# Sparse attention with a mixture of experts: product 1 in seven sub-products, output sums in three halves, sub-products spread over a step

## The chip, the cores and the metric

The kernel runs on one core of a Trainium2 chip. The metric is the time of one execution on the device in microseconds (us): the median of three runs of the kernel before is 2161.44 us, the lowest 2160.73, the highest 2161.88. The core's engines are TensorE (PE in the profile, its weight loads are PEld), VectorE (DVE), ScalarE (ACT), GpSimd (POOL) and SyncE (SP), which here issues nearly all DMAs. PE writes its results into PSUM banks; DVE and ACT read them from there.

## The reference

Block-sparse attention, whose output feeds a mixture of eight experts. The change lies in the second part.

```python
def _moe_ref(x, w_gate, w1, w2):          # x: 3072 x 512, w1: 8 x 512 x 1024, w2: 8 x 1024 x 512
    logits = x @ w_gate
    ...
    out = np.zeros((N, D), dtype=np.float32)
    for e in range(E):
        h = np.maximum(x @ w1[e], 0.0)
        ye = h @ w2[e]
        out += P[:, e:e + 1] * ye
    return out
```

All arrays are float32, and float32 accuracy is kept: each operand is held as a high and a low float16 part, and each product is three matmuls (high by high, high by low, low by high).

## The kernel before

**Items.** The second part runs over 32 items: eight experts times four batches of 768 rows (`NI = NE * B`), item `i` being expert `i // 4`, batch `i % 4`. Stage 1 of an item is `relu(x @ w1)`, stage 2 multiplies by `w2` and adds to the batch's sum. Stage 2 of item i is interleaved with stage 1 of item i+1; the main loop at the end calls that a step, and below it is "a step" too.

**Seven products.** Both stages split their matrices in 2 x 2 blocks and use the seven products of Strassen's method (in Winograd's form) in place of eight. In stage 1 a product, numbered 0 to 6, is made for one quarter `qi` of its output rows at a time: two chunks of the inner dimension times three matmuls, each 128x384. In stage 2 a product is three steps (`ci`) of 4 x 3 matmuls of 128x256.

**Sub-products.** From item 8 on (`FIRST_FINE = 2 * B`) product 0 of stage 1 is itself split by the same method into seven sub-products (`fine`, L1491). A sub-product is six matmuls of 128x192, so product 0 costs 7 x 6 = 42 of these, where in the plain form it takes 4 x 6 = 24 of 128x384. They need sums of blocks of w1 (`w1f_sum`, split into `w1f`, once per expert) and of x (`xpf`, made once per batch by `queue_fine_x` and kept in DRAM as `xfd`). They run one item ahead: those of item i+1 stand between the products of item i, in its last two quarters (`QFINE = 2`), those of item 8 alone at the head of its own stage 1. Their results, the pair `a1` of four blocks, are what the other products are added to.

**The other engines in stage 1.** DVE adds each product's PSUM bank to the running sums (`comb`, L1485). ACT writes the float16 high part of each hidden block `h` (L1596) and the relus; the low part is made by DVE from PSUM (L1601), by DVE for product 4 (L1607), or by POOL for products 2, 5 and 6 (L1607, `LOPE`). POOL also makes four sums per quarter (L1661 and L1298). ACT takes the high parts of those sums from POOL, in program order.

**Order.** A class `Slots` holds work that is waiting and, at every `tick`, releases what its count of costs lets through: urgent work (parts of h, the POOL sums), and lazy work (the weights of the next expert: scaling on ACT, sums on POOL at L1291 and L1316, splits on ACT and DVE at L1276 and L1280). `need` forces work out before its first use. The framework's scheduler then settles the order on each engine; engines run their queue in order.

**DMA.** SP's queue carries, per item, the loads of x blocks (L263, `xp`), of `xpf` (L1425), the store and load of the batch's sum (`keep_acc`, L1169, and `fetch_acc`, L1172; 1536 KB each way) and, per expert, the raw w1 and w2 (L202, 2048 KB each, one buffer for both).

**Buffers.** Eight `upool` tiles for temporaries, three `apool` tiles for the pairs, four PSUM banks for stage 1 (`ps_h`) and four for stage 2 (`ps_y`), two whole sums in SBUF (`accs`).

## Time and profile before

| | |
|---|---|
| median of three runs | 2161.44 us |
| the profiled execution | 2162.28 us, of which its span is 2160.5 us |
| DVE, ACT, POOL busy over the span | 1680.3, 1223.6, 1401.6 us |
| matmuls over the span | 19228 |
| first and last matmul of the sub-products (L1513) | start at 827.5 and 2069.3 us |

The attention part fills roughly the first 470 us; the items follow. The page of the profile gives busy times and shares of the span, then 40 slices of 54 us each, the chain of work that ended last, and the costliest groups; the other views used below are groups by line and shape, waits, windows (busy time of each engine in a stretch) and timelines. A matmul's row in a timeline has its start and a duration that includes its way through the array, so the pace is read from one start to the next.

### The profile page before, as it was taken

To read this page: it belongs to the slowest core of one execution; us is meant where nothing else is said; L and a number is where in the kernel's file an instruction comes from. 1 tells how busy PE (TensorE), PEld (TensorE's weight loads), DVE (VectorE), ACT (ScalarE), POOL (GpSimd) and SP (SyncE) were. 2 spreads that over 40 slices of the span, in tenths; PEclk is the share of its full clock that TensorE was granted. 3 is DMA by queue.
4 is the path that set the end of the run, shared out by engine and by line. 5 is a ranking of instruction groups with operands and counts; after the bars stand their busy time and mean duration, and the time that the engine had idled before them with its cause. 6 is when DMAs were issued, how large, how long until landed. Compare 5 with 4: busy or idle time off the path is not lost.

```text
span 2160.5 us, 48393 instructions
## 1 busy us (share of the span) xinstructions
PE 2126.5 (98%) x19228; PEld 1617.8 (75%) x19228; DVE 1680.3 (78%) x3116; ACT 1223.6 (57%) x2352; POOL 1401.6 (65%) x1550
## 2 busy tenths in 40 slices
PE   6999999999999999999999999999999999999999
PEld 4777776677777777777777777777777777777777
DVE  8889998777867677877787778777877787778765
ACT  5888888666465556554554455445544454455332
POOL 5667778567458675867575747575757575757443
PEclk9999999999999999999999999999999999999999
DMA  6757796143144334343434343434343434343331
GB/s 173 188 128 176 170 209 146 39 138 112 63 154 157 132 125 164 125 156 118 157 118 157 118 157 118 157 118 157 118 157 118 157 118 157 118 157 125 118 104 52
DMA packets 208312, 293.10 MB, mean 136 GB/s; under 512 B 133820, under 2 KB 152276, under 8 KB 200916
## 3 DMA queue, kind: packets, MB, share of 16 engines
q1 hardware_dynamic: 207520, 289.97, 43.0%
q8 instruction: 150, 2.46, 0.5%
q14 instruction: 78, 0.64, 0.1%
q10 hardware_dynamic: 564, 0.03, 0.0%
HBM read 195.59 MB, written 62.91 MB: 120 GB/s over the span
## 4 chain that ended last, share of the span: by engine, by line
PE 88%; DVE 5%; POOL 3%; ACT 2%; issue 1%; DMA 0%; POOLq 0%; ACTq 0%; DVEq 0%
PE py L1712 39%; PE p L1580 34%; PE u L834 3%; PE t L769 2%; PE t L772 2%; PE m L736 2%; PE m L739 2%; DVE top L745 2%; PE fy L1513 2%; PE fz L1513 1%; PE fx L1513 1%; ACT pe L777 1%; DVE vl L645 1%; POOL s L1661 0%; DVE pl L787 0%
## 5 line engine op out<-in xcount | busy, mean ns | idle before, releaser
L1712 PEld LDWEIGHTS <-h 128*128 128x128 f16 x8064 | 787.8, 98 | 144.6 <-issue 0.5
L1712 PE MATMUL py<-w2p,h 128*128 128x256 f16 x4608 | 571.1, 273 | 0.0
L1661 POOL TENSOR_TENSOR s<-a,u 128x384 f32<-128x384 f32 x128 | 146.8, 1147 | 578.1 <-ACT a L1658 578.0
L1736 DVE SCALAR_TENSOR_TENSOR acc<-py,spare,acc 128x256 f32<-128x256 f32 (+1 forms) x588 | 300.4, 515 | 145.5 <-PE py L1712 134.3
L1712 PE MATMUL py<-vault,h 128*128 128x256 f16 x3456 | 410.6, 273 | 0.4 <-DVE vault L1280 0.4
L1596 ACT ACTIVATE h<-p 128x384 f16<-128x384 f32 x384 | 186.4, 485 | 249.6 <-DVE p L1485 249.1
L1580 PEld LDWEIGHTS <-attic 128*128 128x128 f16 x2016 | 196.5, 98 | 105.0 <-issue 0.4
L1601 DVE SCALAR_TENSOR_TENSOR h<-p,h 128x384 f16<-128x384 f32 x384 | 211.2, 550 | 51.0 <-ACT h L1596 20.0
L1485 DVE SCALAR_TENSOR_TENSOR a<-p,a 128x384 f32<-128x384 f32 x384 | 211.1, 550 | 37.9 <-PE p L1580 33.9
L1580 PE MATMUL p<-attic 128*128 128x384 f16 x1152 | 214.9, 326 | 0.2 <-DVE a L1485 0.2
L745 DVE TENSOR_REDUCE top<-m 128x1 f32<-128x768 f32 x192 | 181.9, 950 | 31.1 <-PE m L739 29.9
L777 ACT ACTIVATE pe<-t,qk 128x768 int32<-128x768 f32 x192 | 172.6, 901 | 58.9 <-PE t L772 46.2
L1580 PEld LDWEIGHTS <-arena 128*128 128x128 f16 x1440 | 140.2, 98 | 75.4 <-issue 1.7
L1580 PEld LDWEIGHTS <-w1p 128*128 128x128 f16 x1344 | 131.1, 98 | 69.6
L1485 DVE SCALAR_TENSOR_TENSOR p<-p,u 128x384 f32<-128x384 f32 x256 | 143.0, 559 | 44.6 <-PE p L1580 44.0
L1298 POOL TENSOR_TENSOR r<-s,r 128x384 f32<-128x384 f32 x128 | 155.8, 1217 | 10.0
L1580 PE MATMUL p<-arena,attic 128*128 128x384 f16 x864 | 162.1, 326 | 0.0
L1580 PE MATMUL p<-arena 128*128 128x384 f16 x864 | 158.9, 326 | 1.2 <-DVE a L1485 0.8
L791 POOL TENSOR_SCALAR pl<-pe 128x768 f16<-128x768 uint16 x126 | 109.2, 869 | 67.5 <-ACT pe L777 58.8
L1607 DVE TENSOR_TENSOR h<-s,h 128x384 f16<-128x384 f32 x128 | 112.8, 881 | 40.0 <-ACT h L1596 38.4
L834 PE MATMUL u<-vq,pl 128*128 128x65 f16 x1152 | 142.5, 193 | 1.3 <-POOL pl L791 0.9
L1580 PE MATMUL p<-arena,w1p 128*128 128x384 f16 x768 | 143.7, 326 | 0.0
(236 smaller groups left out, 4312.1 us busy)
## 6 DMA issues: line engine op xcount, KB each, us to landing
arena<-xd SPq DMA_DIRECT2D x128, 384.0 KB, 3.9
accd<-acc SPq DMA_DIRECT2D x28, 1536.0 KB, 5.8
acc<-accd SPq DMA_DIRECT2D x28, 1536.0 KB, 6.4
attic<-xd SPq DMA_DIRECT2D x96, 384.0 KB, 3.7
r<-in_moe_w_dram SPq DMA_DIRECT2D x14, 2048.0 KB, 9.0
xpf<-xfd SPq DMA_DIRECT2D x24, 384.0 KB, 3.1
arena<-in_q_dram SPq DMA_DIRECT2D x16, 384.0 KB, 4.2
arena<-in_k_dram SPq DMA_DIRECT2D x16, 384.0 KB, 4.7
```

The lines of the kernel that those rows point to most:

```text
L745: nc.vector.tensor_reduce(out=tops[n][:, c : c + 1], in_=sc[:, :S], axis=AX.X, op=ALU.max)
L777: nc.scalar.activation(pe, sc[:, :S], AF.Exp, bias=EXP_SHIFT, scale=qk[n // 2][3])
L834: nc.tensor.matmul(uv[:, c, :n], lhsT=l[:, c * P : (c + 1) * P], rhs=w[:, h, kc, :n], start=(kc == 0 and c == 0 and m == 0), stop=(kc == N ...
L1298: nc.gpsimd.tensor_tensor(out=out, in0=x, in1=y, op=ALU.subtract)
L1485: nc.vector.scalar_tensor_tensor(out=t, in0=ps, scalar=HDOWN, in1=other, op0=ALU.mult, op1=ALU.add)
L1580: nc.tensor.matmul(ps, lhsT=w1ps[i // B][p][:, l, kc, fs], rhs=xp[p][:, r, kc], start=(kc == 0 and m == 0), stop=(kc == KH - 1 and m == 2),)
L1596: nc.scalar.activation(h[:, 0], src, AF.Relu if relu else AF.Copy)
L1601: nc.vector.scalar_tensor_tensor(out=h[:, 1], in0=src, scalar=0.0, in1=h[:, 0], op0=ALU.max, op1=ALU.subtract,)
L1607: eng.tensor_tensor(out=h[:, 1], in0=src, in1=h[:, 0], op=ALU.subtract)
L1661: nc.gpsimd.tensor_tensor(out=s1, in0=a1, in1=u3, op=ALU.add)
L1712: nc.tensor.matmul(py, lhsT=hs[i, p, kc][:, l, tsl], rhs=w2p[p][:, r, kc], start=(old is None and kc == 0 and m == 0), stop=(kc == KF // 2 ...
L1736: nc.vector.scalar_tensor_tensor(out=dst, in0=src, scalar=c, in1=dst, op0=ALU.mult, op1=ALU.add)
```

## The change

Four things are done.

**Product 1 too is made of seven sub-products** from item 8 on, also one item ahead. `fine` now has 14 steps: seven for product 0 (PSUM banks `fx`, `fy`, `fz`) and seven for product 1 (`gx`, `gy`, `gz`). The result of product 1 lies in a new pool `rpool` (three tiles), started by three additions on POOL (`base`: the first sub-product plus product 0's blocks) and finished by six `comb`s on DVE. Stage 1 of an item then begins with the relu of that result and the high part of h for product 0, both on ACT, and has five products per quarter in place of six; the low part for product 0 goes from DVE to POOL (`lop`). Four more sums of w1 per expert on POOL (into the tile `s3` that is free by then), one more split into `w1f_1`, twice as many block sums of x (made in items 2 to 5 in place of 4 to 7). The two products' inputs `xpf` share one tile: `load_pieces(i, 1)` is issued after step 5 (sub-product 4 of product 0), and step 9 (sub-product 5 of product 1) is its first reader.

**The sub-products are spread** over a step by the table `BETWEEN`: one or two after a named product of quarters 1 to 3. Item 8's own run in the step before, from blocks that `load_first` brings into two tiles that are free then.

**The sums lie in three halves**: `accs` has three tiles of half a sum, two for the lower halves and one for all upper halves. The upper half is stored after product 4 of stage 2, its last writer, and the next batch's upper half is fetched right behind; 768 KB each.

**Room**: `upool` has six tiles, since the temporaries for product 1 are gone.

```diff
-NU = 8
+NU = 6
...
-    FINE_P = NP
+    FINE_P = (NP, NP + 1)
...
-    xfd = [dram.tile([P, 2, 4, TQ], F16, name=f"xfd_{b}") for b in range(B)]
+    xfd = [
+        [dram.tile([P, 2, 4, TQ], F16, name=f"xfd_{b}_{p}") for p in range(2)]
+        for b in range(B)
+    ]
...
+    rpool = mpool("rpool", 3)
...
-    accs = [big.tile([P, NC, DM], F32, name=f"acc_{b}") for b in range(2)]
+    accs = [big.tile([P, CH, DM], F32, name=f"acc_{n}") for n in range(3)]
...
     def acc(t):
-        return accs[t // NC % 2][:, t % NC]
+        b, c = divmod(t, NC)
+        return accs[2 if c >= CH else b % 2][:, c % CH]
+
+    def move_acc(b, j, keep):
+        out_, in_ = accd[b][:, j * CH : (j + 1) * CH], accs[2 if j else b % 2]
+        if not keep:
+            out_, in_ = in_, out_
+        nc.sync.dma_start(out=out_, in_=in_)
...
-        finer["w"] = right.tile([P, 2, 4, FQ], F16, name="w1f")
+        finer["w"] = [right.tile([P, 2, 4, FQ], F16, name=f"w1f_{p}") for p in range(2)]
...
         one(0, a[0, 0])
+        fine_sums(0, tmps[0], a[0, 0])
         if e == 2:
-            split_finer()
+            split_finer(0)
         queue_sum(a[0, 0], a[1, 0], a[0, 0], ("w1", e, 5))
         one(1, a[0, 1])
+        one(6, s3)
+        fine_sums(1, tmps[1], a[0, 1])
         queue_sum(a[0, 1], a[0, 1], a[0, 0], ("w1", e, 2))
-        one(6, s3)
+        if e == 2:
+            split_finer(1)
...
-    def load_fine(i):
-        nc.sync.dma_start(out=xp[0], in_=xd[i % B][:, 0])
-        nc.sync.dma_start(out=finer["x"], in_=xfd[i % B])
+    def load_pieces(i, p):
+        nc.sync.dma_start(out=finer["x"], in_=xfd[i % B][p])
...
+        product1 = pieces(1)
+        bx, t0 = bank_("gx"), fresh("s0")
+        product1(0, bx, True)
+        nc.scalar.activation(t0, two(bx), AF.Copy, scale=HDOWN)
+
+        def base(f, t):
+            nc.gpsimd.tensor_tensor(
+                out=at_(sums_, f, t), in0=t0, in1=at_(pair, f, t), op=ALU.add
+            )
+
+        base(1, 0)
+        base(1, 1)
+        tick(0, 1, 1.9)
+        yield
         product(2, bz, False)
-        comb(part(0, 1), two(bz), t5)
-        if used:
-            used[0]()
-            used[FINE_P]()
-        if i + 1 < NI:
-            load_fine(i + 1)
+        comb(t5, two(bz), t5)
+        last(0)
+        base(0, 1)
+        tick(1, 0, 0.95)
+        yield
+        product1(1, bx, False)
+        comb(at_(sums_, 0, 0), two(bx), at_(pair, 0, 0))
         tick(1, 0)
         yield
+        by, t5, t6 = bank_("gy"), at_(sums_, 0, 1), at_(sums_, 1, 1)
+        for n, (p, f, t) in enumerate(((5, 0, 1), (6, 1, 1), (3, 1, 0))):
+            product1(p, by, n == 0)
+            comb(at_(sums_, f, t), two(by), at_(sums_, f, t))
...
+        bz = bank_("gz")
+        product1(4, bz, True)
+        if i + 1 < NI:
+            load_pieces(i + 1, 0)
+        comb(t6, two(bz), t6)
...
+        product1(2, bz, False)
+        comb(t5, two(bz), t5)
+        last(1)
...
+    BETWEEN = {
+        (1, 4): 1, (1, 2): 1, (2, 5): 1, (2, 6): 1, (2, 3): 1, (2, 4): 2, (2, 2): 2,
+        (3, 5): 1, (3, 6): 1, (3, 3): 1, (3, 4): 1, (3, 2): 1,
+    }
...
-        lop = LOPE if i < NLE else LOP
+        plain = i < FIRST_FINE
+        lop = LOPE if plain else (0,) + LOPE
...
         else:
-            a1 = pairs[i][qi // 2][:, qi % 2]
-        r11 = fresh("r11")
-        p2 = product(1)
-        comb(p2, p2, a1)
-        emit(0, p2, relu=True)
-        nc.scalar.activation(r11, p2, AF.Relu)
-        tick(1, 2)
-        yield
+            a1, r11 = (x[qi // 2][:, qi % 2] for x in pairs[i])
+            nc.scalar.activation(r11, r11, AF.Relu)
+            emit(0, r11)
...
-        if i == FIRST_FINE:
-            for _ in fine(i, swap(i)):
-                yield 3
-        ahead = fine(i + 1, swap(i + 1)) if FIRST_FINE <= i < NI - 1 else None
+        ahead = fine(i + 1, swap(i + 1)) if FIRST_FINE <= i + 1 < NI else None
         for qi in range(FH // P):
-            for _ in stage1(i, qi, swap(i) if qi == FH // P - 1 else None):
-                yield 2
-                if ahead and qi >= QFINE and next(ahead, "end") != "end":
+            if qi == 1 and i + 1 == FIRST_FINE:
+                load_first()
+            for p in stage1(i, qi, swap(i) if qi == FH // P - 1 else None):
+                yield 1
+                for _ in range(BETWEEN.get((qi, p), 0) if ahead else 0):
+                    next(ahead)
                     yield 0
...
             yield from stage2(i, p)
+            if p == 4 and e + 1 < NE:
+                move_acc(b, 1, True)
+            if p == 4 and B <= i + 1 < NI:
+                move_acc((b + 1) % B, 1, False)
...
-        if B <= i < 2 * B:
-            queue_fine_x(i - B)
         if i == 2:
             finish_late()
+        if 2 <= i < 2 + B:
+            for p in range(2):
+                queue_fine_x(i - 2, p)
...
-            keep_acc(b)
+            move_acc(b, 0, True)
```

Order on POOL. The first place is in the step that runs stage 1 of item 18 (expert 4, batch 2), at the turn from quarter 1 to quarter 2; the raw w1 of expert 5 is being summed there. In the names `a1`, `u3`, `c21`, `s1`, `r11` or `r1` the numbers are item and quarter (for `a1` and `r1` item and half), `h_n` is a hidden block's tile, L1291/L1296, L1316/L1321 are sums of w1, and L1607/L1691 low parts. Before:

```order
L1298 TENSOR_TENSOR c21_18_1_20487<-c21_18_1_20487,r11_18_1_20414 128x384
L1607 TENSOR_TENSOR h_12_8126<-r11_18_1_20414,h_12_8126 128x384
L1607 TENSOR_TENSOR h_21_8135<-c21_18_1_20487,h_21_8135 128x384
L1291 TENSOR_TENSOR r1_5_20213<-r1_5_20213 128x512
L1316 TENSOR_TENSOR w1f_sum_9932<-r1_5_20213 128x256 x2
L1316 TENSOR_TENSOR w1f_sum_9932<-w1f_sum_9932,r1_5_20213 128x256
L1316 TENSOR_TENSOR w1f_sum_9932<-r1_5_20213,w1f_sum_9932 128x256
L1291 TENSOR_TENSOR r1_5_20213<-r1_5_20213 128x512 x2
L1661 TENSOR_TENSOR s1_18_2_20731<-a1_18_1_19904,u3_18_2_20612 128x384
```

In the changed kernel, from the same row to the same row:

```order
L1303 TENSOR_TENSOR c21_18_1_20826<-c21_18_1_20826,r1_18_0_20223 128x384
L1691 TENSOR_TENSOR h_26_8147<-r1_18_0_20223,h_26_8147 128x384
L1691 TENSOR_TENSOR h_1_8122<-c21_18_1_20826,h_1_8122 128x384
L1691 TENSOR_TENSOR h_27_8148<-r1_18_1_20330,h_27_8148 128x384
L1321 TENSOR_TENSOR w1f_sum_9936<-r1_5_20595 128x256
L1321 TENSOR_TENSOR w1f_sum_9936<-w1f_sum_9936,r1_5_20595 128x256
L1612 TENSOR_TENSOR r1_19_1_21033<-s0_19_21066,a1_19_1_21032 128x2x192 x2
L1321 TENSOR_TENSOR w1f_sum_9936<-r1_5_20595,w1f_sum_9936 128x256
L1296 TENSOR_TENSOR r1_5_20595<-r1_5_20595 128x512
L1612 TENSOR_TENSOR r1_19_0_20926<-s0_19_21066,a1_19_0_20925 128x2x192
L1750 TENSOR_TENSOR s1_18_2_21086<-a1_18_1_20329,u3_18_2_20971 128x384
```

One low part for product 0 (`h_27`) and the three additions for item 19 (L1612) have come in ahead of the quarter's sums; three of the w1 sums stand elsewhere.

Order on SP. The second place is in the step that runs stage 1 of item 16, around the load of the raw w2 of expert 4 (`r2_4`); `xd_0` are the x blocks of item 16 and `xd_1`, `xd_2` those of items 17 and 18 (`arena` and `attic` are where they go). Before:

```order
L1425 DMA xpf_9934<-xfd_1_82 128x1536
L263 DMA arena_102<-xd_0_77 128x1536
L1424 DMA arena_102<-xd_1_78 128x1536
L263 DMA arena_102<-xd_0_77 128x1536 x2
L263 DMA attic_106<-xd_0_77 128x1536 x3
L202 DMA r2_4_18993<-in_moe_w2_dram 128x8x512
L1169 DMA accd_2_87<-acc_0_8144 128x3072
L1172 DMA acc_0_8144<-accd_0_85 128x3072
```

In the changed kernel:

```order
L266 DMA attic_110<-xd_0_77 128x1536 x2
L1177 DMA acc_2_8153<-accd_3_92 128x1536
L1437 DMA xpf_9939<-xfd_1_0_83 128x1536
L205 DMA r2_4_19318<-in_moe_w2_dram 128x8x512
L266 DMA attic_110<-xd_0_77 128x1536
L1177 DMA accd_2_91<-acc_0_8151 128x1536
L266 DMA arena_106<-xd_1_78 128x1536
L1177 DMA acc_0_8151<-accd_0_89 128x1536
L1437 DMA xpf_9939<-xfd_1_1_84 128x1536
```

The last x block of item 16 (the one for product 2) now stands behind the 2048 KB of w2, and the sums move in halves; `xpf` is loaded twice per item.

More of the change, by code (lines that the diff above doesn't have):

```diff
@@ L1466, in low @@
             Pinned.vector.tensor_tensor(
-                out=st[:, 1, part], in0=flat(sums_)[:, part], in1=st[:, 0, part],
+                out=st[:, 1, part], in0=made["flat"][:, part], in1=st[:, 0, part],
                 op=ALU.subtract,
@@ L1471, in low @@
                 nc.sync.dma_start(
-                    out=xfd[b].rearrange("p l n t -> p l (n t)"), in_=st
+                    out=xfd[b][p].rearrange("p l n t -> p l (n t)"), in_=st
                 )
@@ L1508, in bank_, with pieces, product @@
             return ps_h.tile([P, 512], F32, tag="ph", name=f"{nm}_{i}")[:, :TH]
-        def product(p, ps, first):
-            for f in range(2):
-                for m, (l, r) in enumerate(((0, 0), (0, 1), (1, 0))):
-                    nc.tensor.matmul(
-                        ps[:, f * TQ : (f + 1) * TQ],
-                        lhsT=ws[p][:, l, f * P : (f + 1) * P], rhs=xs[p][:, r],
-                        start=first and f == 0 and m == 0, stop=f == 1 and m == 2,
-                        skip_group_check=True,
-                    )
+        def pieces(p):
+            slots.need(("w1", e, p))
+            slots.need(("w1", e, FINE_P[p]))
+            w, x = w1ps[e][p], (first_x if i == FIRST_FINE else xp)[p]
+            w1f, xpf = finer["w"][p], finer["x"]
+            ws = {
+                0: w[:, :, 0, :FQ], 1: w[:, :, 1, :FQ], 3: w[:, :, 1, FQ:],
+                6: w1f[:, :, 0], 4: w1f[:, :, 1], 5: w1f[:, :, 2], 2: w1f[:, :, 3],
+            }
+            xs = {
+                0: x[:, :, 0, :TQ], 1: x[:, :, 1, :TQ], 2: x[:, :, 1, TQ:],
+                4: xpf[:, :, 0], 6: xpf[:, :, 1], 5: xpf[:, :, 2], 3: xpf[:, :, 3],
+            }
+            def product(n, ps, first):
+                for f in range(2):
+                    for m, (l, r) in enumerate(((0, 0), (0, 1), (1, 0))):
+                        nc.tensor.matmul(
+                            ps[:, f * TQ : (f + 1) * TQ],
+                            lhsT=ws[n][:, l, f * P : (f + 1) * P], rhs=xs[n][:, r],
+                            start=first and f == 0 and m == 0, stop=f == 1 and m == 2,
+                            skip_group_check=True,
+                        )
+            return product
@@ L1520, in fresh, with last, tick @@
+        def last(p):
+            if used:
+                used[p]()
+                used[FINE_P[p]]()
+            if FIRST_FINE < i < NI - 1:
+                load_x1(i + 1, p)
         def fresh(nm):
             return two(upool.tile([P, TH], F32, tag="u", name=f"{nm}_{i}"))
-        pair = pairs[i] = [
-            finer["a"].tile([P, 2, TH], F32, tag="a", name=f"a1_{i}_{n}") for n in range(2)
-        ]
-        def part(f, t):
-            return pair[f][:, :, t * TQ : (t + 1) * TQ]
-        def tick(n, m):
-            slots.tick(0.495, 0.55 * n, 0.5 * m, 0.5)
+        def tick(n, m, k=0.0):
+            slots.tick(0.495, 0.55 * n, 0.5 * m, 0.5, k)
@@ L1533, in fine @@
+        product = pieces(0)
         bx, t0 = bank_("fx"), fresh("t0")
@@ L1537, in fine @@
         yield
+        room(0)
         product(1, bx, False)
-        nc.scalar.activation(part(0, 0), two(bx), AF.Copy, scale=HDOWN)
+        nc.scalar.activation(at_(pair, 0, 0), two(bx), AF.Copy, scale=HDOWN)
         tick(0, 1)
         yield
-        by, t5 = bank_("fy"), fresh("t5")
+        by, t5 = bank_("fy"), at_(pair, 0, 1)
         product(5, by, True)
@@ L1551, in fine @@
         yield
+        room(1)
         product(3, by, False)
-        comb(part(1, 0), two(by), t0)
+        comb(at_(pair, 1, 0), two(by), t0)
         tick(1, 0)
@@ L1688, in tile_sparse_attention_moe @@
     DONE = {0: (0, 0), 3: (1, 0), 4: (1, 1), 2: (0, 1)}
-    sums = {}
+    sums, firsts = {}, {}
     def stage2(i, p):
```

151 lines of the change are left out of this document (85 added, 66 removed).

## The prediction

> **What bounds the kernel now.** The page comes first: the span, PE's busy time, the slices of PE, POOL and the granted clock, and the chain that ended last.
>
> ```profile
> span 2160.5 us, 48393 instructions
> PE 2126.5 (98%) x19228; PEld 1617.8 (75%) x19228; DVE 1680.3 (78%) x3116; ACT 1223.6 (57%) x2352; POOL 1401.6 (65%) x1550
> ...
> PE   6999999999999999999999999999999999999999
> ...
> POOL 5667778567458675867575747575757575757443
> PEclk9999999999999999999999999999999999999999
> ...
> PE 88%; DVE 5%; POOL 3%; ACT 2%; issue 1%; DMA 0%; POOLq 0%; ACTq 0%; DVEq 0%
> ```
>
> PE is busy for 98% of the span at full clock and has 88% of the chain; POOL alternates between 5 and 7 tenths. Next, the windows, cut at the start of the items (470) and at the first sub-products (827). The columns are length, PE, PEld, DVE, ACT, POOL, clock, DMA share, GB/s.
>
> ```profile
> 470.00:827.00 357.00, 355.86 (x2761) 267.72 (x2759) 271.28 (x529) 205.42 (x436) 242.22 (x243) 1.00 0.38 126
> 827.00:2080.00 1253.00, 1252.06 (x10100) 971.98 (x10099) 960.06 (x1792) 626.99 (x1322) 804.91 (x806) 1.00 0.40 136
> ```
>
> Of 1253 us with sub-products PE lacks one; nearly all its idle time lies in the attention part, which the change leaves alone. So in the items each microsecond of PE work removed is a microsecond gained, as long as no other engine makes PE wait. The answer for the sub-products' line says how close that is: all that PE has waited ahead of them, over 24 items.
>
> ```profile
> its engine sat idle before it (us, times) until:
>   issue: 0.8, 1
>   ACT t L1535: 0.6, 1
> ```
>
> **What PE saves.** The pace is read from starts in PE's timeline.
>
> ```profile
> 1020.76 1.14 PE L1580 MATMUL p<-arena,w1p 128*128 128x384 f16 x6
> 1021.74 1.14 PE L1580 MATMUL p<-arena,attic 128*128 128x384 f16 x6
> 1022.71 1.47 PE L1712 MATMUL py<-w2p,h 128*128 128x256 f16 x12
> 1024.02 0.66 PE L1513 MATMUL fx<-arena 128*128 128x192 f16 x6
> 1024.52 0.66 PE L1513 MATMUL fy<-xpf,w1f 128*128 128x192 f16 x6
> 1025.01 1.14 PE L1580 MATMUL p<-attic,w1p 128*128 128x384 f16 x6
> ...
> 1031.05 0.66 PE L1513 MATMUL fz<-xpf,w1f 128*128 128x192 f16 x6
> 1031.55 0.66 PE L1513 MATMUL fy<-xpf,arena 128*128 128x192 f16 x6
> 1032.04 1.91 PE L1712 MATMUL py<-w2p,h 128*128 128x256 f16 x16
> ```
>
> A plain product of one quarter takes 0.976 us (1020.76 to 1022.71 is two), a part of stage 2 takes 1.31, a sub-product 0.49 to 0.495 (both pairs take 0.99); half of a plain one would be 0.488. I take 0.493. An item then is 24 x 0.976 + 7 x 0.493 + 21 x 1.31 = 54.4 us. Product 1 goes from 4 x 0.976 = 3.90 us to 7 x 0.493 = 3.45: 0.453 us less per item, for the 24 items from 8 to 31 **10.9 us** (10.5 to 11.7 by 0.495 and 0.488). Product 0 is untouched and only moves.
>
> **The other engines.** POOL gets most of the new work. Its load in two whole items, one with sums of w1 and one without, and the groups that are nearest to the new operations:
>
> ```profile
> 936.10:990.60 54.50, 54.50 (x442) 42.32 (x441) 40.95 (x79) 30.90 (x67) 41.63 (x40) 1.00 0.34 117
> 990.60:1045.00 54.40, 54.40 (x441) 42.25 (x439) 42.53 (x75) 24.39 (x50) 29.96 (x28) 1.00 0.35 117
> ```
>
> ```profile
> L1661 POOL TENSOR_TENSOR s<-a,u 128x384 f32<-128x384 f32 x92 | 107.5, 1168 | 431.2 <-ACT a L1658 431.1
> ...
> L1298 POOL TENSOR_TENSOR c<-c,r 128x384 f32<-128x384 f32 x92 | 92.6, 1007 | 1.4
> L1607 POOL TENSOR_TENSOR h<-r,h 128x384 f16<-128x384 f32 x92 | 88.8, 965 | 0.0
> ...
> L1316 POOL TENSOR_TENSOR w1f_sum<-r 128x256 f32<-128x256 f32 x10 | 12.0, 1216 | 0.0
> L1316 POOL TENSOR_TENSOR w1f_sum<-w1f_sum,r 128x256 f32<-128x256 f32 x5 | 3.6, 728 | 0.4
> L1316 POOL TENSOR_TENSOR w1f_sum<-r,w1f_sum 128x256 f32<-128x256 f32 x5 | 3.6, 726 | 0.4
> ```
>
> Per item come three additions at 1.01 to 1.17 us and four low parts at 0.965: 6.9 to 7.4 us, I take 7.2; per expert four more sums, 2 x 1.216 + 0.73 + 0.73 = 3.9 us. A quiet item goes from 30.0 to 37 us of POOL, a dense one from 41.6 to 41.6 + 7.2 + 3.9 = 52.7, of an item that then lasts 53.9. That still fits, with 1.2 us to spare; the POOL order shown above does what the sum says, seven rows of w1 sums thinned to four where product 1's rows come in. What is late next is the DVE row that adds onto POOL's additions (`gy`), three products behind them.
>
> DVE and ACT change little:
>
> ```profile
> L1596 ACT ACTIVATE h<-p 128x384 f16<-128x384 f32 x316 | 153.4, 485 | 206.7 <-DVE p L1485 206.2
> ...
> L1658 ACT ACTIVATE a<-a 128x384 f32<-128x384 f32 x106 | 55.3, 522 | 57.1 <-DVE a L1485 55.8
> ```
>
> ```profile
> L1601 DVE SCALAR_TENSOR_TENSOR h<-p,h 128x384 f16<-128x384 f32 x316 | 173.8, 550 | 40.2 <-ACT h L1596 17.3 <-ACT r L1632 14.2 <-ACT c L1647 5.5
> L1485 DVE SCALAR_TENSOR_TENSOR a<-p,a 128x384 f32<-128x384 f32 x316 | 173.7, 550 | 31.5 <-PE p L1580 28.4
> ```
>
> ACT had eight reads of product 1 at 0.485 (3.9 us) and gets one at 0.485 and eight from SBUF at 0.522 (4.7); it is busy for 24 to 31 us of an item. DVE had four `comb`s and four low parts (4.4 us) and gets six `comb`s (3.3). The block sums of x, twice as many, fall into items 2 to 5, where POOL has 115 us free of 357. All of it lies beside PE, which costs nothing while the cover holds.
>
> **DMA.** `xpf` has one tile: between step 5 and step 9, which reads it again, `BETWEEN` puts three sub-products, two plain products and 17/20 of a part of stage 2 for each of them: 1.48 + 1.95 + 2.23 = 5.7 us.
>
> ```profile
> L1425 SPq DMA_DIRECT2D xpf<-xfd x24: 319/320/2247, 702.8 to 2011.5; - x24
> ...
> DMA to landing us min/median/max: 2.8/3.1/7.1
> ```
>
> At the median of 3.1 plus 0.3 to issue it is there 2.3 us early; at 7.1 PE waits 1.7. Bounds: 0 to 1.7 per item, I take 0, the median's side. Two more DMAs of the page, with KB each and median us from issue to landing:
>
> ```profile
> acc<-accd SPq DMA_DIRECT2D x28, 1536.0 KB, 6.4
> ...
> r<-in_moe_w_dram SPq DMA_DIRECT2D x14, 2048.0 KB, 9.0
> ```
>
> The upper sums' store and fetch stand behind a wait for DVE in SP's queue; they are half as large as today's 1536 KB and have a whole quarter until their next use. The x block behind the 2048 KB of w2 is first read after four stage 2 parts, four products and three more parts, 13 us: hidden.
>
> What remains is small waits: PE has 1.4 us of them at 168 sub-products; with twice as many, and three sub-product banks alive at once, I add 1 us (0 to 3). **Sum:** 2162.28 - 10.9 + 1.0 = 2152.4 for an execution like the profiled one; the median is 0.84 us below it, so **2151.5 us**.
>
> **The rivals.**
>
> *Weight loads set the pace of narrow matmuls.* Each 128x192 matmul needs its own load:
>
> ```profile
> L1513 PEld LDWEIGHTS <-w1f x576: 97/98/98, 829.3 to 2069.2; 128*128 128x128 f16 x192
> ```
>
> Were loads the bound, product 1 would take 42 x 0.098 = 4.12 us against 3.90, 0.21 more in each of 24 items, and the 10.9 us are not gained: 2151.5 + 10.9 + 5.0 = 2167.4. Against it: the pair from 1031.05 to 1032.04 is twelve such matmuls in 0.99 us, 82 ns each, less than a load. Chance 0.03; longer runs are rare in the new order. [...]
>
> *POOL becomes the bound in the dense items: the slower side.* There are five (w1 of experts 3 to 7), each with 1.2 us spare by my sum and 0.8 us until the `gy` row makes DVE, and with it the PSUM banks, late. It decides from about 2 us more of POOL work per dense item. The price per operation is not fixed:
>
> ```profile
> 982.94 0.91 POOL L1607 TENSOR_TENSOR h<-a,h 128x384 f16<-128x384 f32 x1
> ...
> 995.80 1.89 POOL L1607 TENSOR_TENSOR h<-a,h 128x384 f16<-128x384 f32 x1
> ```
>
> ```profile
> 995.30 1.62 DVE L1280 SCALAR_TENSOR_TENSOR w1f<-w1f_sum,sw,w1f 128x1024 f16<-128x1024 f32 x1
> ```
>
> The second took 1 us longer and ended 0.8 us after DVE's split of w1f. If the seven new operations of a dense item cost 1.9 each, that is 6.3 us more, 4.3 past both margins; five items make 21.5 us: 2173. Against it: in the dense item quoted above POOL was busy for 41.63 us, and PE for all of the 54.50. Chance 0.08. [...]
>
> *A wait for a bank takes the place of the work removed.* `gx`, `fz` and two plain products hold all four banks at the end of quarter 2. At the 0.6 us that PE once waited for ACT, in every item, 24 x 0.6 = 14.4 us stand in place of the 1 us of small waits: 2164.9, no change. Against it: the same point has three banks in use now and one wait in 24 items. Chance 0.07.
>
> *`xpf` comes late behind the raw w1.* 1.7 us at each of five experts, 8.5 at most, half of it likely: 2155.8. Chance 0.08.
>
> That sub-products are not made in place of product 1 is excluded: the order has 42 `gx`, `gy`, `gz` matmuls per item.
>
> **Numbers.** The forecast has 0.74. About 0.2% (4.3 us) is what a measurement can tell: faster means below 2157.1, and holds forecast and `xpf` rival, 0.82; no change is the bank rival, 0.07; slower are POOL and weight loads, 0.11. The range goes from 2148.3 (2151.5 less 0.8 for the saving's other end, 1.0 for the small waits added and 1.4 for today's) to 2160.0 (the `xpf` rival at its full 8.5; the 2 us by which small waits could be longer lie inside). It leaves out banks, POOL and weight loads, 0.18.
>
> **What would show it.** Right: from item 8 on an item of 53.9 us in place of 54.4, no PE wait above 1 us among the sub-products, POOL near 37 us in quiet items and 52 in dense ones, six matmuls of 128x192 in 0.49 us also in `gx` to `gz`. Wrong: waits of PE for DVE or ACT in the five dense items (POOL), ahead of `gx` or `fz` in every item (banks), ahead of `gy` with a DMA as releaser (`xpf`), or a pace above 0.5 us (weight loads).

## The result, and the profile after

| | before | after |
|---|---|---|
| median | 2161.66 us (4 runs) | 2186.65 us (2185.5 to 2188.21, 4 runs) |
| ratio | | 1.0115, 95% interval 1.0098 to 1.0133 |
| span of the profiled run | 2160.5 us | 2184.8 us |

The change makes the kernel **25 us slower**; the forecast was 2151.5, the range 2148.3 to 2160.0. The page of the changed kernel, with its span, its busy times, POOL's slices and the chain that ended last:

```profile
span 2184.8 us, 49326 instructions
...
PE 2124.3 (97%) x19660; PEld 1644.7 (75%) x19660; DVE 1662.7 (76%) x3082; ACT 1241.0 (57%) x2386; POOL 1623.0 (74%) x1766
...
POOL 5667778567668786878687868786878687868763
...
PE 71%; POOL 15%; DVE 7%; ACT 4%; issue 3%; DMA 1%; POOLq 0%; ACTq 0%; DVEq 0%
```

POOL's share of the chain went from 3% to 15%, at a load of 74%: no engine but PE is full. The window of the items with sub-products shows PE's loss, 25.7 us of idle time where there was one:

```profile
827.00:2080.00 1253.00, 1227.35 (x10320) 980.12 (x10318) 921.67 (x1725) 634.09 (x1337) 982.81 (x966) 1.00 0.41 141
```

The view of PE's waits names those that are new (total, times, longest):

```profile
PE py L1801 <- DVE acc L1823: 7.9, 6, 1.3
...
PE fx L1552 <- ACT t L1576: 7.0, 11, 1.2
...
PE p L1664 <- DVE h L1685: 5.7, 7, 1.0
...
PE py L1801 <- DVE vault L1285: 2.9, 6, 0.5
...
PE fy L1552 <- DVE a L1513: 2.2, 5, 0.4
```

The counts are the first clue: five, six or eleven (seven with two that lie in items before), as many as there are experts whose weights are made ready during these items, not 24. So this is not a price that each item pays.

**What PE lost and saved.** The waits of this view start at the modelled end of a matmul and are 0.15 to 0.17 us short each. I therefore add up, over PE's timeline, the time from each row's start to the next, less 0.0823, 0.1092 or 0.1625 us for each matmul of 192, 256 or 384 columns: the paces by the starts, where nothing waits (12 of 192 in 0.99 us from 1031.05 in the kernel before; 33 of 256 in 3.60 from 1348.27 and 24 of 384 in 3.90 from 1334.04 in the changed one). From the first stage 2 matmul (at 418 us) to PE's last:

| | length | waits | work | waits before the first sub-product |
|---|---|---|---|---|
| before | 1738.5 | 3.5 | 1735.0 | 2.1 |
| after | 1762.1 | 38.4 | 1723.7 | 5.7 |

The work fell by 11.3 us, the waits grew by 34.9. The waits lie at two places of each expert. Four windows of one expert, 55.5 us each, show POOL's busy time there (columns as before: length, PE, PEld, DVE, ACT, POOL):

```profile
1190.00:1245.50 55.50, 55.10 (x466) 44.18 (x465) 41.58 (x75) 26.69 (x50) 49.08 (x47) 1.00 0.36 121
1245.50:1301.00 55.50, 53.25 (x447) 42.33 (x447) 40.30 (x74) 28.09 (x61) 37.90 (x38) 1.00 0.47 160
1301.00:1356.50 55.50, 54.73 (x462) 43.60 (x460) 41.90 (x84) 28.68 (x63) 47.05 (x49) 1.00 0.34 122
1356.50:1412.00 55.50, 54.16 (x458) 43.36 (x457) 39.08 (x75) 28.58 (x66) 41.99 (x42) 1.00 0.47 160
```

The first is the dense item with the sums of w1, the third has those of w2; PE's waits stand at the ends of these two and the starts of the next.

**Place 1: the sums of w2.** POOL's timeline (start, length):

```profile
1341.81 3.78 POOL L1296 TENSOR_TENSOR r<-r,t 128x256 f32<-128x256 f32 x4
1345.55 0.91 POOL L1691 TENSOR_TENSOR h<-c,h 128x384 f16<-128x384 f32 x1
1346.42 4.05 POOL L1296 TENSOR_TENSOR r<-r 128x256 f32<-128x256 f32 x3
1350.44 1.01 POOL L1750 TENSOR_TENSOR s<-a,u 128x384 f32<-128x384 f32 x1
```

ACT's, with what ended its idle time:

```profile
1342.88 0.52 ACT L1747 ACTIVATE a<-a 128x384 f32<-128x384 f32 x1
1345.62 1.15 ACT L1281 ACTIVATE vault<-r,sw 128x1024 f16<-128x1024 f32 x1 [2.22 <-POOL r L1296]
1351.48 0.52 ACT L1680 ACTIVATE h<-s 128x384 f16<-128x384 f32 x1 [4.71 <-POOL s L1750]
1351.91 0.47 ACT L1680 ACTIVATE h<-p 128x384 f16<-128x384 f32 x1
1352.28 0.48 ACT L1736 ACTIVATE c<-p 128x384 f32<-128x384 f32 x1
1352.65 0.49 ACT L1576 ACTIVATE t<-fx 128x384 f32<-128x384 f32 x1
```

And PE's:

```profile
1348.27 3.76 PE L1801 MATMUL py<-vault,h 128*128 128x256 f16 x33 [0.47 <-DVE vault L1285]
1351.87 1.14 PE L1664 MATMUL p<-attic 128*128 128x384 f16 x6
1353.19 0.49 PE L1552 MATMUL fx<-arena,w1p 128*128 128x192 f16 x4 [0.18 <-ACT t L1576]
...
1362.16 0.71 PE L1801 MATMUL py<-w2p,h 128*128 128x256 f16 x5 [1.33 <-DVE acc L1823]
```

Read them from POOL up: the sum `s` could start at 1343.4, when ACT's `a` was done, and starts 7.0 us later behind the sums of w2. ACT takes its queue in order and stands 4.71 us before `s`, though PE has filled the PSUM banks `p` and `fx` that come behind it by 1348. PE gets `vault`, the new w2, late and then waits for `fx` and `acc`: 2.8 us for one expert, six times. In these items of the kernel before POOL's `s` started at most 0.4 us behind its input, 0.1 on average; here at most 7.0, 0.9 on average.

**Place 2: the sums of w1**, at the turn into an expert's first item. POOL, ACT and PE:

```profile
1224.66 4.72 POOL L1691 TENSOR_TENSOR h<-r,h 128x384 f16<-128x384 f32 x3
...
1234.43 4.55 POOL L1296 TENSOR_TENSOR r<-r 128x512 f32<-128x512 f32 x2
1238.94 1.01 POOL L1750 TENSOR_TENSOR s<-a,u 128x384 f32<-128x384 f32 x1
```

```profile
1235.25 0.52 ACT L1747 ACTIVATE a<-a 128x384 f32<-128x384 f32 x1
...
1239.99 0.53 ACT L1680 ACTIVATE h<-s 128x384 f16<-128x384 f32 x1 [3.41 <-POOL s L1750]
...
1248.23 0.49 ACT L1576 ACTIVATE t<-fx 128x384 f32<-128x384 f32 x1
```

```profile
1246.12 1.14 PE L1664 MATMUL p<-arena,attic 128*128 128x384 f16 x6 [1.01 <-DVE h L1685]
...
1248.77 0.66 PE L1552 MATMUL fx<-arena,w1p 128*128 128x192 f16 x6 [1.18 <-ACT t L1576]
```

`s` is 3.2 us late, ACT passes it on, and PE waits 1.19, 1.35 and 0.60 us by its starts: 3.1 for each of five experts. Six times 2.8, five times 3.1 and the 5.7 before the first sub-product make 38.0 of the 38.4.

### The profile page after: what moved, and what is told of

It reads as the page before. It is cut to its first block, busy times and chain, and to the rows that moved or that the text cites. A ratio compares the mean times of both kernels' runs of the same rounds, so it can differ in the third digit from the quotient of the medians.

```text
span 2184.8 us, 49326 instructions
## 1 busy us (share of the span) xinstructions
PE 2124.3 (97%) x19660; PEld 1644.7 (75%) x19660; DVE 1662.7 (76%) x3082; ACT 1241.0 (57%) x2386; POOL 1623.0 (74%) x1766
## 4 chain that ended last, share of the span: by engine, by line
PE 71%; POOL 15%; DVE 7%; ACT 4%; issue 3%; DMA 1%; POOLq 0%; ACTq 0%; DVEq 0%
PE py L1801 31%; PE p L1664 23%; POOL r L1296 3%; POOL h L1691 3%; PE u L837 3%; DVE top L748 2%; POOL s L1750 2%; PE t L772 2%; PE t L775 2%; PE m L739 2%; PE m L742 2%; PE gy L1552 1%; PE fy L1552 1%; POOL r L1303 1%; POOL a L1303 1%
## 5 line engine op out<-in xcount | busy, mean ns | idle before, releaser
L1801 PE MATMUL py<-w2p,h 128*128 128x256 f16 x4608 | 578.1, 273 | 8.6 <-DVE acc L1823 7.9
L1691 POOL TENSOR_TENSOR h<-r,h 128x384 f16<-128x384 f32 x224 | 238.3, 1068 | 19.5 <-ACT h L1680 19.5
L1664 PEld LDWEIGHTS <-attic 128*128 128x128 f16 x1824 | 177.2, 98 | 94.0 <-issue 3.3
L1680 ACT ACTIVATE h<-p 128x384 f16<-128x384 f32 x288 | 139.5, 484 | 136.7 <-DVE p L1513 136.3
L1685 DVE SCALAR_TENSOR_TENSOR h<-p,h 128x384 f16<-128x384 f32 x288 | 159.3, 553 | 62.7 <-ACT h L1680 29.4
L1664 PEld LDWEIGHTS <-w1p 128*128 128x128 f16 x1248 | 121.3, 98 | 63.8 <-issue 2.2
L1691 DVE TENSOR_TENSOR h<-s,h 128x384 f16<-128x384 f32 x128 | 106.3, 830 | 78.7 <-ACT h L1680 77.7
L1680 ACT ACTIVATE h<-s 128x384 f16<-128x384 f32 x128 | 66.6, 521 | 174.6 <-POOL s L1750 174.5
L1680 ACT ACTIVATE h<-r 128x384 f16<-128x384 f32 x224 | 114.3, 519 | 90.0 <-POOL r L1303 71.4
L1664 PEld LDWEIGHTS <-arena 128*128 128x128 f16 x1152 | 112.1, 98 | 61.2 <-issue 2.6
```

Of the source, the lines that this page charges most:

```text
L1664: nc.tensor.matmul(ps, lhsT=w1ps[i // B][p][:, l, kc, fs], rhs=xp[p][:, r, kc], start=(kc == 0 and m == 0), stop=(kc == KH - 1 and m == 2),)
L1680: nc.scalar.activation(h[:, 0], src, AF.Relu if relu else AF.Copy)
L1685: nc.vector.scalar_tensor_tensor(out=h[:, 1], in0=src, scalar=0.0, in1=h[:, 0], op0=ALU.max, op1=ALU.subtract,)
L1691: eng.tensor_tensor(out=h[:, 1], in0=src, in1=h[:, 0], op=ALU.subtract)
L1801: nc.tensor.matmul(py, lhsT=hs[i, p, kc][:, l, tsl], rhs=w2p[p][:, r, kc], start=(old is None and kc == 0 and m == 0), stop=(kc == KF // 2 ...
```

## The experiments

Theories. **A**: POOL has too much work, and PE waits behind it. **B**: three banks of sub-products leave too few for the plain products. **C**: the sub-products' new place, from quarter 1 on, costs PE by itself. **D**, formed after the eighth run: it is a matter of *when* the planner releases the sums of weights; the changed kernel releases them late, and sums and splits pile up before their deadline. **E**: for one surprise, below. The runs were made in five groups (e1 to e4, e5 to e8, e9 to e12, e13 and e14, e15 and e16) on four chips, each group beside the kernel before on the same chip (2161.57 to 2161.99 us):

| run | edit | median, us | ratio to before, 95% |
|---|---|---|---|
| e1 | after, low of product 0 on DVE | 2176.52 | 1.0055 to 1.0085 |
| e2 | after, `base` on DVE | 2186.47 | 1.0094 to 1.0128 |
| e3 | after, planner's prices | 2180.80 | 1.0074 to 1.0104 |
| e4 | after, sub-products in quarters 2, 3 | 2159.56 | 0.9980 to 0.9999 |
| e5 | e1 and e3 | 2171.50 | 1.0026 to 1.0060 |
| e6 | before, sub-products from quarter 1 | 2163.82 | 1.0002 to 1.0021 |
| e7 | before, low of product 4 on POOL | 2170.22 | 1.0024 to 1.0054 |
| e8 | e4 and e3 | **2153.95** | 0.9952 to 0.9978 |
| e9 | after, first w2 sums free of charge | 2218.95 | 1.0248 to 1.0279 |
| e10 | e4, w2 sums held back | 2173.55 | 1.0039 to 1.0069 |
| e11 | e9 and a price for w1 | 2197.46 | 1.0145 to 1.0179 |
| e12 | e8, block sums of x later | 2154.11 | 0.9951 to 0.9977 |
| e13 | e11 and e1 | 2205.39 | 1.0171 to 1.0207 |
| e14 | e8 and e1 | 2161.83 | 0.9989 to 1.0008 |
| e15 | after, one pause shorter | 2169.79 | 1.0022 to 1.0047 |
| e16 | e15 and a price for w1 | **2154.86** | 0.9954 to 0.9980 |

**First: which part of the change?**

```diff
e1  -        lop = LOPE if plain else (0,) + LOPE
    +        lop = LOPE
e2  -            nc.gpsimd.tensor_tensor(
    +            nc.vector.tensor_tensor(
                     out=at_(sums_, f, t), in0=t0, in1=at_(pair, f, t), op=ALU.add
```

> The changed kernel with one line undone: the low part of product 0 is made by DVE again, as before the change, so POOL has four operations of 0.9 to 1.1 us less per item. Theory A (POOL is late at two places of each expert, and ACT, which takes its queue in order, holds PSUM banks while it waits for POOL's sum s): at the turn into an expert's first item the row of three lows of r ahead of the w1 sums (4.72 us) shrinks by about 2.8, near the whole 3.2 us by which s is late there, and of six w2 sums forced per expert four remain; most of the 5.9 us of PE waits per expert go: 2150 to 2162 us. Theory B (three banks of sub-products alive at once leave too few for the plain products, whatever POOL does): the waits stay, 2183 to 2190 us.

> The changed kernel with the three additions that start product 1's blocks made by DVE in place of POOL. POOL has three operations of 1.0 to 1.1 us less per item, and none of them stands in the two bursts. Theory A with the bursts as the cause: the forced w2 sums fall from six to two per expert, so the waits around the w2 sums (2.8 us per expert) shrink, those at the w1 sums (3.1 us) stay: 2165 to 2178 us. If POOL's total load were the cause whatever its order, it would do about three quarters of what the low part of product 0 does. Theory B: 2183 to 2190 us.

e1, 2176.5, lies between the two forecasts. At the w1 sums `s` is late no more and the waits there are gone, as A says; at the w2 sums `s` is still 4.3 us late and PE's waits are 3.5 us per expert, not less. e2 misses A's range and lies in B's: no `s` is over 2 us late any more, and the time does not move; PE now waits for `fx` at the w2 sums, 3.2 us by its starts. So a late `s` is not the whole of place 1.

```diff
e3  -                key, 1, True, pool=4.0 / n if n > 2 else 1.7,
    +                key, 1, True, pool=0.73 if n > 2 else 1.27,
e4  -        (1, 4): 1, (1, 2): 1, (2, 5): 1, (2, 6): 1, (2, 3): 1, (2, 4): 2, (2, 2): 2,
    -        (3, 5): 1, (3, 6): 1, (3, 3): 1, (3, 4): 1, (3, 2): 1,
    +        (2, 5): 1, (2, 6): 1, (2, 3): 1, (2, 4): 2, (2, 2): 2,
    +        (3, 5): 1, (3, 6): 1, (3, 3): 2, (3, 4): 2, (3, 2): 1,
```

> The changed kernel with other prices in the planner alone: 0.73 and 1.27 us for a sum of weights of 256 and 512 columns (the durations of the trace) in place of 1.0 and 1.7. POOL does the same work, only the order changes: no w2 sum is forced by its deadline any more. Theory A with the forced row as the cause: the 2.8 us per expert around the w2 sums go (about 16 us), those at the w1 sums at most shrink: 2155 to 2172 us. If POOL's total load is the cause: no change, 2183 to 2190 us. Theory B: no change.

> The changed kernel with its fourteen sub-products in quarters 2 and 3 alone, as the seven stood before, in place of quarters 1 to 3. Theory A: no POOL sum is forced here either, so the waits around the w2 sums go; the w1 sums are not touched: 2155 to 2175 us. Theory B: the sub-products stand closer together, their three banks are handed on faster, and the waits grow: 2186 to 2200 us.

e3 takes the waits at the w1 sums away by order alone, against the theory of a total load; those at the w2 sums stay (3.5 us per expert, ahead of `fx`; on ACT three splits of 1.15 us stand in front of its reader). The time, 2180.8, lies between the two forecasts. e4 is the large one, 27 us, inside A's range, though it only takes two of the fourteen sub-products out of quarter 1 and lets the rest follow that much later. It rules B out, since it puts them closer together.

**Second: the early place, POOL's load, or both?**

```diff
e6  -            for _ in stage1(i, qi, swap(i) if qi == FH // P - 1 else None):
    +            for n, _ in enumerate(stage1(i, qi, swap(i) if qi == FH // P - 1 else None)):
                     yield 2
    -                if ahead and qi >= QFINE and next(ahead, "end") != "end":
    +                if ahead and (qi, n) >= (1, 4) and next(ahead, "end") != "end":
e7  -LOPE = (2, 5, 6)
    +LOPE = (2, 4, 5, 6)
```

e5 joins the edits of e1 and e3, e8 those of e3 and e4.

> The changed kernel with the edits of both the first and the third experiment: product 0's low part on DVE, and the measured prices for the sums of weights in the planner. No w2 sum is forced, and POOL has four operations less per item. Theory A (POOL's lateness alone makes PE wait): nothing is late any more, 2151 to 2157 us. Theory C (at the w2 sums of each expert the sub-products now stand in quarter 1, their bank's reader on ACT stands behind three splits of 1.15 us and behind POOL's s, and the second sub-product into that bank must wait for the reader, even if POOL is on time): a wait of 3 us or more ahead of fx stays in each of six experts, 2166 to 2178 us.

> The kernel before with one edit: its seven sub-products of product 0 begin in quarter 1 behind product 4, at the very place where the changed kernel's begin, in place of quarter 2. No product 1 in pieces, no added work for any engine. Theory C: the wait of about 3 us ahead of fx at the w2 sums comes up in the kernel before too, six times: 2172 to 2185 us. Theory A (added POOL work is needed for it): 2160 to 2166 us.

> The kernel before with one edit: the low part of product 4 is made by POOL in place of DVE, four operations of 0.9 to 1.1 us more per item on POOL, as many as the changed kernel adds with product 0's low part; the sub-products stay in quarters 2 and 3. Six w2 sums per expert are then forced by their deadline, as in the changed kernel. Theory A: s runs several us late at the w2 sums, PE waits there, 2166 to 2178 us. Theory C (the early sub-products are needed for it): 2160 to 2165 us.

> The changed kernel with the sub-products in quarters 2 and 3 (as in the fourth experiment) and the measured prices for the sums of weights in the planner. If the 1.2 us per expert of waits that the fourth experiment kept come from the order of the sums, they go: 2152 to 2156 us. If they come from the density of sub-products at the turn of items: 2158 to 2161 us, no change from the fourth.

e6 refutes C for the kernel before: the early place alone costs 2 us where C said 10 or more. e7 costs 8.6 us and lies in A's range, but by luck: `s` is never more than 1.0 us late there, and at the w2 sums of five of the six experts PE waits 0.2 us at most. 4.9 us of its waits stand at one place (886 to 908 us), 4.9 before the first sub-product, where the kernel before has 2.1. Its forecast had six w2 sums per expert forced; as the program is built, the planner forces three, and it releases the first of the sums when the kernel before does. So e7 does not test A at the places in question. e5 lies in C's range, but C's sign, a wait ahead of `fx` at the w2 sums, is not there: PE waits 2.0 us in each of six experts, now for ACT's split of `vault`. e8 has no wait of PE left from item 8 on, and is **7.6 us faster than the kernel before**, 2.5 us above the forecast for the change.

Neither A nor C explains all of this, but e4 and e3 have one thing in common: both change when the planner lets sums of weights go, e4 those of w2, e3 most of all those of w1. Its own clock, as the program is built, for the first eight w2 sums of one expert (us of PE work; their deadline is at 1335.4, that of the other eight at 1347.2), and how many of all sixteen a deadline forces:

```
after  1328.1 1329.4 1329.4 1330.9 1332.2 1332.7 1335.4 1335.4   6 forced
e4     1314.8 1314.8 1314.8 1316.3 1317.3 1328.9 1330.4 1331.7   0
e8     1314.8 1314.8 1314.8 1315.3 1316.3 1316.8 1317.3 1328.9   0
e10    1328.4 1328.4 1329.4 1330.4 1331.7 1332.7 1335.4 1335.4   6 forced
e15    1314.5 1314.5 1314.5 1315.8 1317.3 1317.8 1329.9 1330.9   0
```

In the changed kernel the last step of the scale of w2, which the sums are queued behind, is released at 1317.3 in place of 1314.8, as sub-products of quarter 1 are already charged. By the next time that the queue could move, product 1's three additions and the sums of stage 1 are charged to POOL; the account stays full until 1328. So 2.5 us of delay become 13. This is theory D.

The traces show the delay on the chip too. Here a point in time is given as PE work: the sum of the paces above over all matmuls that have started since the first stage 2 matmul, so that waits do not shift it (its zero is not that of the planner's clock). The place is the first w2 sum of expert 4 on POOL; the waits are PE's around the w2 sums, per expert:

| run | first w2 sum starts at PE work of | PE waits there |
|---|---|---|
| e4, e8, e15, e16 | 856.1 us | under 0.2 us |
| e10 | 871.2 us | 2.2 us |
| after, e2, e3 | 872.5 us | 2.8, 3.2, 3.5 us |
| e1, e5 | 888.9 us | 3.5, 2.0 us |
| e9 | 886.6 us | 5.5 us |

e3 forces no sum by its deadline and keeps these waits, so it is the late start that counts, not the forcing. A late start alone does not make PE wait either: the kernel before starts at 873.8 and e14, with four operations less per item on POOL, at 871.0, and they wait under 0.2 and 0.5 us. It takes the late start and the change's work beside it.

**Third: D from the side of the late sub-products.** e10 is e4 with only the release put back:

```diff
+    def queue_sum(out, x, y, key, op=ALU.subtract, delay=1, pool=None):
...
-                queue_sum(t1, m[0, 1], m[0, 0], ("scale", 2, e))
+                queue_sum(t1, m[0, 1], m[0, 0], ("scale", 2, e), delay=24)
```

> The changed kernel with its sub-products in quarters 2 and 3 (as in the fourth experiment, 2159.6 us), and with the w2 sums held back by a delay so that they are released at the same counts as in the changed kernel, with the same six forced by their deadline. Theory D: the waits around the w2 sums come back though no sub-product stands there, 2.8 us in each of six experts: 2170 to 2180 us. Theory C: nothing comes back, 2157 to 2163 us.

D holds: 14.0 us come back, most of them in waits of PE for `acc` at the w2 sums (six experts, two each), ahead of the first sub-product of that item:

```profile
PE py L1802 <- DVE acc L1824: 8.2, 12, 0.7
```

**Fourth: D from the side of the early sub-products; a miss.** e11 adds 1.27 in place of 1.7 for a sum of w1 of 512 columns, e13 adds e1.

```diff
e9  -                queue_sum(t1, m[0, 1], m[0, 0], ("scale", 2, e))
    -                queue_sum(m[0, 1], m[0, 1], m[1, 1], ("scale", 2, e))
    +                queue_sum(t1, m[0, 1], m[0, 0], ("scale", 2, e), pool=0.0)
    +                queue_sum(m[0, 1], m[0, 1], m[1, 1], ("scale", 2, e), pool=0.0)
```

> The changed kernel, its sub-products from quarter 1 on as they are, but with the first eight w2 sums of each expert free of charge in the planner, so that they are released some 9 us of PE work earlier (where the kernel with sub-products in quarters 2 and 3 has them) and no w2 sum is forced. Same work on every engine. Theory D (the early sub-products fill the planner's account of POOL, the w2 sums start about 13 us later, and sums and splits on POOL, ACT and DVE pile up ahead of their deadline): the 2.8 us per expert around the w2 sums go, the 3.1 us at the w1 sums stay: 2166 to 2174 us. Theory C (the place of the sub-products itself, beside the added work): the waits stay, 2182 to 2190 us.

> The ninth experiment and one price more: 1.27 us in place of 1.7 for a sum of w1 of 512 columns, so that the w1 sums too are released earlier. The sub-products stay spread from quarter 1 on, every engine has the changed kernel's work. If both places are a matter of when the sums are released: 2152 to 2160 us. If spreading itself costs: above 2166 us.

> The eleventh experiment (2197.46 us) with product 0's low part on DVE, as in the first. In the eleventh a DVE subtraction of two SBUF tiles (the low part of product 4) took 8.1 us in place of 0.9, six times, while POOL's instructions followed each other without a gap from its start to its end; the lows of product 0 on POOL stood in that row between the sums and took the place of the pauses of 0.08 us that an instruction has which reads the result of the one before. Theory E (DVE's subtraction waits for a pause in POOL's row): without these lows the row is broken, no low part takes over 3 us, and about 43 us go: 2150 to 2160 us. If the 8.1 us come from something else (the place in the program, DMA traffic): 2188 to 2198 us.

All three miss. e9 and e13 are slower than every range in their texts; e11 lies where its text has "If spreading itself costs". Their premise did not hold on the chip: the w2 sums did not come earlier, though the planner let them go earlier. They start at a PE work of 886.6 us in e9 and e11 and 887.2 in e13, 14 us later than in the changed kernel. In us from the start, the changed kernel's row first, then that of e9, which by then has lost 16 of the 30 us between them to waits:

```profile
1311.38 2.78 POOL L1296 TENSOR_TENSOR t<-r 128x256 f32<-128x256 f32 x4
```

```profile
1341.67 3.77 POOL L1296 TENSOR_TENSOR t<-r 128x256 f32<-128x256 f32 x4
```

Why the scheduler placed them so is open. They stand in one unbroken row on POOL, 25 us long in e9 and e11, once 31 (20.7 in the changed kernel, 10.2 at this place in the kernel before). Two new things happened. PE's granted clock fell for some time behind these places, to 0.50 in e9 and e13 (views in the last section): its mean over the profiled runs was 0.992 in e9, 0.993 in e11 and 0.991 in e13, by their spans of 2219.9, 2198.9 and 2204.4 us an estimated 15 to 20 us of the time. And a subtraction on DVE became very long; DVE in e9, and POOL at the same time:

```profile
1354.33 8.13 DVE L1692 TENSOR_TENSOR h<-s,h 128x384 f16<-128x384 f32 x1 [1.14 <-ACT h L1681]
1362.38 0.55 DVE L1514 SCALAR_TENSOR_TENSOR u<-p,a 128x384 f32<-128x384 f32 x1
```

```profile
1353.62 1.41 POOL L1296 TENSOR_TENSOR r<-r 128x256 f32<-128x256 f32 x2
1354.99 0.91 POOL L1692 TENSOR_TENSOR h<-r,h 128x384 f16<-128x384 f32 x1
...
1361.14 0.91 POOL L1692 TENSOR_TENSOR h<-r,h 128x384 f16<-128x384 f32 x1
1367.58 0.92 POOL L1692 TENSOR_TENSOR h<-c,h 128x384 f16<-128x384 f32 x1 [5.53 <-ACT h L1681]
```

A subtraction of 0.9 us took 8.1: it ended at 1362.46, 0.41 us after POOL's row (1362.05). This came six times in e9 and five times in e11, not six as the text on e13 has it. In e13, which takes the lows of product 0 out of that row, no subtraction of DVE is over 1.4 us, as E said; but the 43 us did not go, since the row is still 21 us long and PE waits for `h`, `vault` and `w2p` at the same place. E is not shown by this: at its sixth place in e11 the subtraction took 1.12 us (at 1347.30) with those lows still on POOL, in the middle of the unbroken row of 31 us. So these three do not test D in the way that was meant: their sums came later, not earlier. That they wait longer at this place goes with D, but the slow clock and the long subtraction are mixed into it.

**Fifth: D again, with a release like e4's.** Only a pause in the queue is shortened, for w2 alone; e16 adds the price of w1:

```diff
e15  -        slots.add(spread, key, 1, True, gap=5)
     +        slots.add(spread, key, 1, True, gap=2 if which == 2 else 5)
e16  -                key, 1, True, pool=4.0 / n if n > 2 else 1.7,
     +                key, 1, True, pool=4.0 / n if n > 2 else 1.27,
```

> The changed kernel, sub-products from quarter 1 on, with one number changed: a pause of two counts in place of five between two steps of the scale of w2, so that its last step, and the w2 sums behind it in the queue, come 2.5 counts earlier, ahead of product 1's additions. Six of the sums are then released at planner times 1314.5 to 1317.8 (the kernel with sub-products in quarters 2 and 3 of the fourth experiment: five at 1314.8 to 1317.3; the changed kernel: from 1328.1 on), and none is forced. Theory D (late release, then a pile at the deadline): the waits at the w2 sums go, 2.8 us in each of six experts, and those at the w1 sums stay: 2166 to 2173 us. Theory C (the place of the sub-products costs it beside the splits, whenever the sums are released): 2180 to 2190 us.

> The fifteenth experiment with one price more: 1.27 us in place of 1.7 for a sum of w1 of 512 columns. Theory D with the w1 sums as the third experiment showed them (their waits gone by the prices): both places are free, 2151 to 2158 us with the sub-products spread as the change has them. If spreading costs anything by itself: 2160 us or more. If the price of 512 columns was not what took the waits at the w1 sums away in the third: as the fifteenth, 2166 to 2173 us.

Both land inside D's range. In e15 the waits at the w2 sums are gone, those at the w1 sums stand unchanged:

```profile
PE fx L1552 <- ACT t L1576: 5.9, 5, 1.2
PE p L1664 <- DVE h L1685: 5.9, 7, 1.0
...
PE fy L1552 <- DVE a L1513: 2.2, 5, 0.4
```

In e16 PE is never idle in the items with sub-products, with the work that the change gives POOL and with its sub-products where the change puts them:

```profile
827.00:2080.00 1253.00, 1253.00 (x10606) 1006.94 (x10604) 942.89 (x1767) 644.31 (x1367) 965.65 (x988) 1.00 0.43 145
```

So the place of the sub-products and POOL's added work cost PE no wait by themselves: two numbers of the planner make up the 32 us between 2186.65 and 2154.86.

**Sixth: what more there is to gain.** e14 joins the edits of e8 and e1; e12 adds to e8:

```diff
e12  -        if 2 <= i < 2 + B:
     -            for p in range(2):
     -                queue_fine_x(i - 2, p)
     +        for p in range(2):
     +            if 2 <= i - p < 2 + B:
     +                queue_fine_x(i - p - 2, p)
```

> The eighth experiment (2153.95 us, all of whose waits of PE, 6.4 us against 3.3 in the kernel before, lie in items 0 to 7), with the block sums of x for product 1 made one item later, in items 3 to 6 in place of 2 to 5. If those waits come from the doubled block sums of x in items 2 to 5: 2 to 3 us less, 2150.5 to 2152.5 us. If not: 2153 to 2155 us.

> The eighth experiment (sub-products in quarters 2 and 3, measured prices, 2153.95 us) with product 0's low part on DVE. The eighth has no wait of PE from item 8 on, so by all theories that time POOL by its lateness there is nothing to gain: 2153 to 2156 us. If POOL's total load cost anything by itself: 2144 to 2150 us, as the same edit brought 9 to 10 us twice with the early sub-products.

e12 (the queue of product 1's x blocks one item later) changes nothing; what makes items 0 to 7 wait about 4 us longer than before is **open**. e14 is a miss worth keeping: the edit that brought 10 us in e1 costs 8 here. With POOL on time DVE and ACT are the next to be late: from item 8 on PE waits 6.0 us where e8 has 0.2, of which 2.3 for DVE's additions ahead of `gy`, 1.5 for ACT and 1.1 for `xpf`. The other 2 us of the 8 are not traced to a wait. The sign of an edit depends on which queue is late.

## Why the prediction was wrong

- *What bounds the kernel* was right: PE's waits and work together make the whole difference (34.9 - 11.3 = 23.6; the spans differ by 24.3, the rest lies ahead of the first stage 2 matmul and behind PE's last).
- *What PE saves* was right: 10.9 us forecast, 11.3 measured as work. In e16 an item takes 53.98 us (215.9 us from one expert's first `gx` to the next's), against the forecast 53.9; in the kernel before it takes 54.40, so by this count 24 items save 10.1 us. Sub-products of product 1 have the pace of the others, 0.49 us for six, where six loads of 98 ns would take 0.59, so weight loads do not set it.
- *The other engines* is the step that failed. Its loads were near or too high: 52.7 us of POOL in the dense item, 49.1 measured; 37 in the quiet one, 37.9 measured. But "that still fits, with 1.2 us to spare" compares a sum with an item's length. POOL is 88% busy in that item and idle at other times of it, while `s`, which ACT and through ACT the PSUM banks wait for in order, is 3.2 us late at one point. The item with the w2 sums, six times in the kernel, was not looked at at all; it holds the largest part of the waits, six times 2.8 or 16.8 of 38.4 us.
- The order was read, its release was not: that starting two sub-products a quarter earlier would shift the sums of w2 by 13 us of PE work appears in neither a load nor a price. The "small waits" term, 1 us, is the term that was mis-sized: 34.9.
- *The POOL rival* (0.08, 2173) named the right engine and the right direction, with the wrong mechanism: it needed POOL to be full over an item, in five dense items, and "what is late next" was DVE's `gy` row. What was late next was ACT's queue. Its price was borne out: in the changed kernel, as in the prediction's rows, sums of w2 are stretched beside DVE's splits. Six of the 28 below took 1.7 us, each beside a split, the others 0.73; the mean is 0.937 us in place of 0.726:

```profile
L1291 POOL TENSOR_TENSOR r<-r,t 128x256 f32<-128x256 f32 x28 | 19.5, 726 | 0.0
```

```profile
L1296 POOL TENSOR_TENSOR r<-r,t 128x256 f32<-128x256 f32 x28 | 25.4, 937 | 0.0
```

(the first row is of the kernel before, the second of the changed one).

- *The bank rival* foresaw waits for ACT ahead of `fx`, but in each of 24 items; they come at the two places alone. *`xpf`*: its DMA takes 4.9 us to land, not 3.1, and PE never waits for it in the changed kernel.

## What to carry to other kernels

Before moving work in a program with a planner, compare when its deferred work is released and what its deadlines force, not only the order and the loads. An engine at 75% (POOL here: 74% of the span) can be the bound at one point of a period: follow the one result that an in-order queue stands before, and look at every kind of period, here the item with w2 too. Where deferred work is late, release it earlier before taking work away; taking it away can make the next engine late, as the fourteenth run shows. And after such an edit look at where the work stands on the chip: in e9 it was released earlier and ran later.
